# Sign bits of a weight block by a product with zero in bfloat16, and the mix's coefficient columns on GpSimd

## The chip, the core and the metric

The kernel runs on one core of a Trainium2 chip. The metric is the device time of one launch in microseconds; it took 817.42 us, the median of three runs (813.95 to 818.76). The engines are called PE (TensorE), DVE (VectorE), ACT (ScalarE), POOL (GpSimd) and SP (SyncE, which issues all DMAs here). Each engine takes its instructions strictly in the order of its own queue and waits on semaphores for the others.

## The reference

Eight batches, eight heads, 576 tokens, 64 features for a head. First a causal attention with a forgetting bias, then a channel mix over the 512 features of all heads:

```
bias   = min(-(cum_i - cum_j), 0), cum = cumsum(max(s, 0))
attn   = softmax(q k^T / 8 + bias, causal);  x = attn v, heads side by side
x_prev = x one token earlier
xk = mu_k x + (1 - mu_k) x_prev;  xr = mu_r x + (1 - mu_r) x_prev
out = sigmoid(xr w_r) * (relu(xk w_k)^2 w_v)
```

q, k, v, s and mu are float32; the three weights (512 x 1024, 1024 x 512, 512 x 512) are float64.

## The kernel before

**Attention.** A visit handles one batch and one pair of heads. The first visits (batch 0, cut in two tile groups A and Z) use plain float32 products; from batch 1 on each float32 operand is split in two parts, and POOL makes most of these parts (KH, KL, QL and G tiles, lines 1132 to 1165). Visits of batches 0 and 1 turn the softmax weights on PE, later visits turn float16 parts by DMA.

**Weights.** `load_weight` (line 813) brings a block of 128 rows and 512 columns of a weight into SBUF as raw float64 words; there are 8 blocks of w_k, 4 of w_r and 8 of w_v. A float32 is then put together from bits. Line 855 (POOL) makes the upper exponent bits from the top byte of each word, as the even 16-bit halves of a tile `last3`; line 863 (POOL) makes the sign bit as the odd halves; line 871 (ACT) and line 876 (DVE) bring the lower part into PSUM and clamp it, with the row maximum beside it; line 883 (DVE) shifts it, combines it with `last3` by a bitwise or, and has the float32 block. `split` then writes two float16 halves: the high one on ACT (line 894) or POOL (line 899), the low one on DVE (line 907) or, in two instructions, on POOL (lines 913 and 917).

**Coefficients.** The mix uses float16 halves too, so its operands are scaled. `set_range(w)` (line 701, w = 0 for k and 1 for r) multiplies mu and 1 − mu by the row maxima (`shares`, line 706), finds their maximum over all partitions through PE, and makes `mu_late` (line 738), the columns that later batches use. `set_group_mu(g, w)` (line 768) makes `group_mu` (named mu_g, line 770) for token groups 0 to 2, from `shares`, `ranges` and the group's `scale`. Each is a tile of 128 partitions and 4 or 8 elements. The readers of mu_g are the mix lines 1877 to 1893 of the first chunks, the readers of mu_late lines 1520 and 1530.

**Channel mix.** 18 chunks of 256 tokens each: mixed operands in a ring, hidden products (line 1949), the gate (line 2012), the output products (line 2057).

**The order of the work.** Nothing is emitted directly. Every operation becomes a task with an engine, a time that the program's own table gives it (`dve`, `act`, `pool`, `pe`, `dma`, lines 390 to 423: elements times a rate plus an extra), and the buffers that it reads and writes. Some tasks carry an alternative on another engine (`or_pool`, `or_dve`, `or_act`). `Plan.run` (line 322) plays a list schedule forward and backward 60 times and keeps the order with the shortest planned end; so a changed engine or a changed number for one task can move tasks on all engines. Until the first split attention product the plan puts filler matmuls (line 450) where PE would have nothing to do.

Of the kernel before, what the change touches and what calls it, by code (L numbers as in the profile page):

```python
# [337 lines left out]
def forgetting_attention_then_channel_mix(  # L338
# [362 lines left out]
    def set_range(w):  # L701
        name = "kr"[w]
        x = most[name]
        for y in range(2):
            dve(
                lambda y=y: nc.vector.tensor_tensor(
                    out=shares.ap[:, w, y], in0=mu.ap[:, w, y], in1=x.ap[:, :, 2], op=ALU.mult
                ),
                [(mu, w), (mu, 2)] + [(x, (c, "m")) for c in range(NC)], [(shares, (w, y))], NC,
            )  # L710
        dve(
            lambda: nc.vector.tensor_reduce(
                out=tops.ap[:, w : w + 1], in_=shares.ap[:, w].rearrange("p y c -> p (y c)"),
                axis=mybir.AxisListType.X, op=ALU.max, apply_absolute_value=True,
            ),
            [(shares, (w, 0)), (shares, (w, 1))], [(tops, w)], 2 * NC,
        )
        ps = spread(lambda: tops.ap[:, w : w + 1], (tops, w))

        def own(i):  # L720
            return ranges.ap[:, w, i : i + 1]

        dve(
            lambda: nc.vector.tensor_reduce(
                out=own(0), in_=ps.get()[:, 0:P], axis=mybir.AxisListType.X, op=ALU.max,
            ),
            [ps], [(ranges, w)], P,
        )
        dve(power(lambda: own(1), lambda: own(0), False), [(ranges, w)], [(ranges, (w, "p"))], 1)
        dve(  # L730
            lambda: nc.vector.tensor_scalar(
                out=own(1), in0=own(1), scalar1=4.0, scalar2=None, op0=ALU.mult,
            ),
            [], [(ranges, (w, "p"))], 1,
        )
        dve(lambda: nc.vector.reciprocal(own(2), own(1)), [(ranges, (w, "p"))], [(ranges, (w, "i"))], 1)
        dve(
            lambda: nc.vector.tensor_scalar(
                out=mu_late.ap[:, w], in0=shares.ap[:, w], scalar1=own(2), scalar2=1.0 / HALF,
                op0=ALU.mult, op1=ALU.mult,  # L740
            ),
            [(ranges, (w, "i")), (shares, (w, 0)), (shares, (w, 1))], [(mu_late, w)], 2 * NC,
        )

    def set_scale(g, tops_of, keys):
# [20 lines left out]
        dve(lambda: nc.vector.reciprocal(own(1), own(0)), [(x, 0)], [(x, 1)], 1)  # L766

    def set_group_mu(g, w):
        dve(
            lambda: nc.vector.tensor_scalar(  # L770
                out=group_mu[g].ap[:, w], in0=shares.ap[:, w], scalar1=ranges.ap[:, w, 2:3],
                scalar2=scale[g].ap[:, 1:2], op0=ALU.mult, op1=ALU.mult,
            ),
            [(ranges, (w, "i")), (shares, (w, 0)), (shares, (w, 1)), (scale[g], 1)],
            [(group_mu[g], w)], 2 * NC,
        )

    def set_gate(g):
# [34 lines left out]
    def load_weight(name, c, o, w, due, x):  # L813
# [34 lines left out]
        top = most[name]  # L848
        column = top.ap[:, c, o : o + 1] if name != "v" else top.ap[:, c : c + 1]

        def short(i):
            return last3.get().bitcast(mybir.dt.int16)[:, i:1024:2]

        pool(
            lambda: nc.gpsimd.tensor_scalar(
                out=short(0),
                in0=words.get().bitcast(mybir.dt.uint8)[:, 3 : 4096 : 8],
                scalar1=1.0 / 32.0, scalar2=-31.0 / 64.0, op0=ALU.mult, op1=ALU.add,
            ),
# [1 line left out]
        )  # L861
        pool(
            lambda: nc.gpsimd.tensor_scalar(
                out=short(1),
                in0=words.get().bitcast(mybir.dt.int16)[:, 3 : 2048 : 4],
                scalar1=32768.0, scalar2=0.0, op0=ALU.mult, op1=ALU.min,
            ),
            [words], [(last3, 1)], 512, 210, 1.0,
        )
# [20 lines left out]
        def split(unit_at, key):  # L890
# [28 lines left out]
                    op=ALU.subtract,  # L919
                )  # L920

            or_pool(dve(low, [whole, key, hi], [lo], 512, extra=260), low_in_two, 512, 1551)
            if name == "v":
                or_dve(
                    act(
# [1442 lines left out]
```

## Time and profile before

| | |
|---|---|
| median of three runs | 817.42 us |
| profiled execution | 817.64 us |
| its span, from first to last instruction | 815.8 us |
| PE busy | 754.2 us (92%) |
| DVE busy | 607.2 us (74%) |
| ACT busy | 568.6 us (70%) |
| POOL busy | 518.3 us (64%) |

Busy shares are means over the whole span. The profile also cuts the span in stretches and gives the busy time, the number of instructions and the granted clock of PE in each; the stretch shows which engine has no idle time left there. A chain of waits is followed back from the last instruction, at each step to whatever released it, so it names the work on which the end depended. Matmuls are pipelined and their ends are modelled, so a nearly full PE can still hold gaps.

### The profile page before, as it was taken

The page shows a single profiled execution, that of the slowest core. Times are in us where ns is not written, and L with a number is a line of the kernel's source. Part 1 is how long each engine was busy: PE and PEld are TensorE (multiplying, and loading weights), DVE is VectorE, ACT ScalarE, POOL GpSimd, SP SyncE. Part 2 cuts the span into 40 slices and gives each one's busy share as a digit, 9 for nine tenths or more (in the row PEclk, how much of TensorE's full clock was granted, in tenths as well). Part 3 has the DMA queues.
Part 4 walks back from the last instruction along what each step waited for, and adds up shares of the span by engine and source line. Part 5 has one row for each costly group of instructions (what it writes and reads, how often), then busy time and mean ns, then how long its engine had stood idle before and what let it go on. Part 6 is the DMA issues. An engine that isn't in the chain of part 4 may idle for free.

```text
span 815.8 us, 16987 instructions
## 1 busy us (share of the span) xinstructions
PE 754.2 (92%) x5400; PEld 503.8 (62%) x5400; DVE 607.2 (74%) x1825; ACT 568.6 (70%) x1716; POOL 518.3 (64%) x606
## 2 busy tenths in 40 slices
PE   9868888879899999998999899999999999999998
PEld 8645666557465666565666565757575656656664
DVE  8757886777998799988888978887887878423321
ACT  6656886757698689978797788887787878312211
POOL 8995999665745658966977598648966873010000
PEclk9989997889999999999999999999999999999999
DMA  8634555415564898897879777958787755300000
GB/s 262 209 100 133 161 173 179 131 43 145 130 127 103 174 158 180 172 202 132 181 167 191 139 183 166 185 122 172 145 184 137 131 110 83 76 14 14 27 27 27
DMA packets 207337, 109.93 MB, mean 135 GB/s; under 512 B 178000, under 2 KB 183888, under 8 KB 207248
## 3 DMA queue, kind: packets, MB, share of 16 engines
q1 hardware_dynamic: 207248, 108.85, 58.7%
q8 instruction: 43, 0.70, 0.4%
q14 instruction: 46, 0.38, 0.2%
HBM read 54.09 MB, written 12.24 MB: 81 GB/s over the span
## 4 chain that ended last, share of the span: by engine, by line
PE 52%; DVE 19%; ACT 11%; POOL 8%; issue 6%; DMA 2%; SPq 1%; DVEq 0%; ACTq 0%; POOLq 0%
PE m L2057 16%; PE m L1949 8%; PE m L2012 7%; PE pp L1475 3%; PE s L1289 3%; DVE W L1347 3%; PE t L1289 2%; ACT W L1341 2%; PE s L1216 2%; PE pp L1699 2%; PE pp L2057 2%; ACT t L1316 2%; PE t L1594 2%; PE t L1949 2%; ACT s L1316 2%
## 5 line engine op out<-in xcount | busy, mean ns | idle before, releaser
L1949 PE MATMUL m<-xkh,w_k 128*128 128x256 f16 x1008 | 188.4, 276 | 9.0 <-DVE kl L1999 8.0
L1949 PEld LDWEIGHTS <-w_k 128*128 128x128 f16 x1728 | 162.8, 99 | 43.2 <-issue 16.5
L2057 PE MATMUL m<-w_v,kh 128*128 128x512 f16 (+1 forms) x544 | 169.3, 377 | 2.5 <-ACT g L2026 1.3
L1949 PE MATMUL m<-xkl,w_k 128*128 128x256 f16 x504 | 139.2, 276 | 0.0
L2057 PE MATMUL m<-w_v,kl 128*128 128x512 f16 (+1 forms) x272 | 102.7, 378 | 1.6 <-DVE w_v L931 1.2
L1136 POOL TENSOR_TENSOR KH<-raw,KH 64x576 fp32r<-64x576 f32 x64 | 91.1, 1424 | 10.4 <-issue 4.7
L2057 PEld LDWEIGHTS <-kh 128*128 128x128 f16 x592 | 56.7, 98 | 65.4 <-issue 12.5
L2031 POOL TENSOR_SCALAR g<-g,scale 128x512 f32<-128x512 f32 x29 | 22.2, 765 | 104.8 <-ACT g L2026 100.2
L1160 POOL TENSOR_TENSOR QL<-raw,G 64x576 fp32r<-64x576 f32 (+1 forms) x64 | 84.5, 1320 | 3.8 <-ACT G L1149 1.0
L2012 PE MATMUL m<-w_r,xrh 128*128 128x512 f16 x240 | 79.6, 391 | 7.7 <-DVE kl L1999 5.2
L1316 ACT ACTIVATE s<-s,nm 128x64 f32<-128x64 f32 (+2 forms) x144 | 61.6, 428 | 27.8 <-DVE nm L1301 24.8
L1347 DVE SCALAR_TENSOR_TENSOR W<-s,rinv,W 128x64 f16<-128x64 f32 (+2 forms) x144 | 65.1, 456 | 14.4 <-ACT W L1341 13.5
L1341 ACT ACTIVATE W<-s,rinv 128x64 f16<-128x64 f32 (+2 forms) x144 | 64.7, 454 | 12.9 <-DVE rinv L1332 11.1
L1289 PE MATMUL s<-KH,G 128*128 128x64 f32 (+3 forms) x192 | 68.9, 362 | 4.0 <-DVE W L1347 3.6
L1962 ACT ACTIVATE r<-m 128x512 f32<-128x512 f32 x61 | 36.5, 598 | 50.8 <-PE m L1949 50.8
L1347 DVE SCALAR_TENSOR_TENSOR W<-t,rinv,W 128x512 f16<-128x512 f32 (+1 forms) x96 | 61.6, 645 | 8.3 <-ACT W L1341 7.7
L1289 PE MATMUL s<-KL,QL 67*128 67x64 f32 (+3 forms) x192 | 67.3, 355 | 0.0
L1156 POOL CAST G<-raw 128x576 fp32r<-128x576 f32 x48 | 31.8, 662 | 52.5 <-issue 24.6
L1316 ACT ACTIVATE t<-t,nm 128x320 f32<-128x320 f32 (+1 forms) x96 | 55.3, 576 | 6.0 <-DVE nm L1378 3.7
L1301 DVE CUSTOM_DVE_ANT_0 t<-t,lower 128x512 f32<-128x512 f32 (+1 forms) x96 | 57.1, 601 | 2.2 <-PE t L1289 1.4
L1341 ACT ACTIVATE W<-t,rinv 128x512 f16<-128x512 f32 (+1 forms) x96 | 57.8, 608 | 1.2 <-DVE rinv L1332 1.1
L1475 PE MATMUL pp<-T,V 128*64 128x512 f16 (+6 forms) x768 | 54.4, 295 | 0.0
(250 smaller groups left out, 1981.2 us busy)
## 6 DMA issues: line engine op xcount, KB each, us to landing
raw<-in_q SPq DMA_DIRECT2D x112, 144.0 KB
raw<-in_k SPq DMA_DIRECT2D x32, 288.0 KB
vn<-in_v SPq DMA_DIRECT2D x24, 384.0 KB
out<-g SPq DMA_DIRECT2D x35, 256.0 KB
wd<-in_moe_w_v SPq DMA_DIRECT2D x8, 512.0 KB
T<-W SPq DMA_TRANSPOSE x192
V<-in_v SPq DMA_DIRECT2D x8, 320.0 KB
wd<-in_moe_w_k SPq DMA_DIRECT2D x4, 512.0 KB
```

The source lines that it names most:

```text
L1136: lambda own=own, other=other, K=K: nc.gpsimd.tensor_tensor(out=K.get()[other], in0=k.get()[own], in1=f32(K.get()[own]), op=ALU.subtract),
L1160: lambda x=x, QQ=QQ, QL=QL: nc.gpsimd.tensor_tensor(out=QL.get()[0:64, 0:nq], in0=x.get()[0:64], in1=f32(QQ.get()[0:64]), op=ALU.subtract,),
L1289: lambda x=x, G=G, K=K, r=r: nc.tensor.matmul(ps.get()[:m, :n], G.get()[:r, q : q + m], K.get()[:r, k0 : k0 + n], start=x == 0, stop=x == 1,),
L1301: lambda: nc.vector.tensor_tensor_reduce(out=ps.get()[:, :n], in0=ps.get()[:, :n], in1=mask(), scale=-SCALE, scalar=3.0e38, op0=ALU.add, o ...
L1316: lambda: nc.scalar.activation(ps.get()[:, :n], ps.get()[:, :n], AF.Exp, bias=nm.get()[:, i + o : i + o + 1], scale=-1.0, accum_out=sums.g ...
L1341: lambda: nc.scalar.activation(part(0), ps.get()[:, :n], AF.Copy, scale=rinv.get()[:, i : i + 1]),
L1347: lambda: nc.vector.scalar_tensor_tensor(out=part(1), in0=ps.get()[:, :n], scalar=rinv.get()[:, i : i + 1], in1=part(0), op0=ALU.mult, op1 ...
L1475: nc.tensor.matmul(ps.get()[64 * j : 64 * j + 64, a:e], V.get()[:, block[0], block[1], j], moving(j), start=first, stop=last, tile_positio ...
L1949: lambda u=u, f=f, c=c, n=n, w=w, x=x: nc.tensor.matmul(ps.get()[:, u * CT : (u + 1) * CT], weight["k", c, f // 4].get()[:, w, f % 4 * P : ...
L1962: lambda: nc.scalar.activation(r.get(), ps.get(), AF.Relu, scale=2.0**-52),
L2012: lambda c=c, n=n, x=x, w=w: nc.tensor.matmul(ps.get(), chunk(1, x, ch).get()[:, c, ts], weight["r", c, 0].get()[:, w], start=c == 0 and n ...
L2057: lambda f=f, i=i, x=x, w=w, ps=ps, columns=columns: nc.tensor.matmul(ps.get()[:, 0:n], x.get()[:, f, ts], weight["v", f, 0].get()[:, w, c ...
```

## The change

The sign bits come from another instruction. Before, POOL read the top 16 bits of each word as int16, multiplied by 32768 and took the minimum with 0, which leaves −32768 (only the sign bit set) for a negative number and 0 otherwise. Now POOL reads the upper 32 bits of each word as a float32, multiplies by 0.0 and writes bfloat16: a negative number gives minus zero, which is the sign bit alone. The tile and the places written are the same. The `shares`, `mu_late` and `mu_g` columns, twelve instructions in all, are tasks of POOL instead of DVE, with an extra of 200. The planner's number for the low half on DVE goes from 260 to 450 (plus 512 elements).

```diff
--- before.py
+++ after.py
@@ -702,11 +702,11 @@
         name = "kr"[w]
         x = most[name]
         for y in range(2):
-            dve(
-                lambda y=y: nc.vector.tensor_tensor(
+            pool(
+                lambda y=y: nc.gpsimd.tensor_tensor(
                     out=shares.ap[:, w, y], in0=mu.ap[:, w, y], in1=x.ap[:, :, 2], op=ALU.mult
                 ),
-                [(mu, w), (mu, 2)] + [(x, (c, "m")) for c in range(NC)], [(shares, (w, y))], NC,
+                [(mu, w), (mu, 2)] + [(x, (c, "m")) for c in range(NC)], [(shares, (w, y))], NC, 200,
             )
         dve(
             lambda: nc.vector.tensor_reduce(
@@ -734,12 +734,12 @@
             [], [(ranges, (w, "p"))], 1,
         )
         dve(lambda: nc.vector.reciprocal(own(2), own(1)), [(ranges, (w, "p"))], [(ranges, (w, "i"))], 1)
-        dve(
-            lambda: nc.vector.tensor_scalar(
+        pool(
+            lambda: nc.gpsimd.tensor_scalar(
                 out=mu_late.ap[:, w], in0=shares.ap[:, w], scalar1=own(2), scalar2=1.0 / HALF,
                 op0=ALU.mult, op1=ALU.mult,
             ),
-            [(ranges, (w, "i")), (shares, (w, 0)), (shares, (w, 1))], [(mu_late, w)], 2 * NC,
+            [(ranges, (w, "i")), (shares, (w, 0)), (shares, (w, 1))], [(mu_late, w)], 2 * NC, 200,
         )
 
     def set_scale(g, tops_of, keys):
@@ -766,13 +766,13 @@
         dve(lambda: nc.vector.reciprocal(own(1), own(0)), [(x, 0)], [(x, 1)], 1)
 
     def set_group_mu(g, w):
-        dve(
-            lambda: nc.vector.tensor_scalar(
+        pool(
+            lambda: nc.gpsimd.tensor_scalar(
                 out=group_mu[g].ap[:, w], in0=shares.ap[:, w], scalar1=ranges.ap[:, w, 2:3],
                 scalar2=scale[g].ap[:, 1:2], op0=ALU.mult, op1=ALU.mult,
             ),
             [(ranges, (w, "i")), (shares, (w, 0)), (shares, (w, 1)), (scale[g], 1)],
-            [(group_mu[g], w)], 2 * NC,
+            [(group_mu[g], w)], 2 * NC, 200,
         )
 
     def set_gate(g):
@@ -848,12 +848,9 @@
         top = most[name]
         column = top.ap[:, c, o : o + 1] if name != "v" else top.ap[:, c : c + 1]
 
-        def short(i):
-            return last3.get().bitcast(mybir.dt.int16)[:, i:1024:2]
-
         pool(
             lambda: nc.gpsimd.tensor_scalar(
-                out=short(0),
+                out=last3.get().bitcast(mybir.dt.int16)[:, 0:1024:2],
                 in0=words.get().bitcast(mybir.dt.uint8)[:, 3 : 4096 : 8],
                 scalar1=1.0 / 32.0, scalar2=-31.0 / 64.0, op0=ALU.mult, op1=ALU.add,
             ),
@@ -861,9 +858,8 @@
         )
         pool(
             lambda: nc.gpsimd.tensor_scalar(
-                out=short(1),
-                in0=words.get().bitcast(mybir.dt.int16)[:, 3 : 2048 : 4],
-                scalar1=32768.0, scalar2=0.0, op0=ALU.mult, op1=ALU.min,
+                out=last3.get().bitcast(BF16)[:, 1:1024:2], in0=word(1),
+                scalar1=0.0, scalar2=1.0, op0=ALU.mult, op1=ALU.mult,
             ),
             [words], [(last3, 1)], 512, 210, 1.0,
         )
@@ -919,7 +915,7 @@
                     op=ALU.subtract,
                 )
 
-            or_pool(dve(low, [whole, key, hi], [lo], 512, extra=260), low_in_two, 512, 1551)
+            or_pool(dve(low, [whole, key, hi], [lo], 512, extra=450), low_in_two, 512, 1551)
             if name == "v":
                 or_dve(
                     act(
```

The lines of the new file are lower by up to four behind the change: 855 is now 852, 863 is 860, 899 is 895, 907 is 903, 913 is 909, 917 is 913, 1054 to 1062 are 1050 to 1058, 1132 is 1128, 1136 is 1132, 1142 is 1138, 1156 is 1152, 1160 is 1156.

First place: POOL's queue where the blocks of w_r are put together. Before:

```order
L855 TENSOR_SCALAR w_r_00_597<-wd_262 128x512
L913 TENSOR_SCALAR xrh_286<-xrh_286,unit 128x512
L917 TENSOR_TENSOR w_k_10_593<-xrh_286,w_k_10_593 128x512
L855 TENSOR_SCALAR w_r_00_643<-wd_210 128x512
L863 TENSOR_SCALAR w_r_00_643<-wd_210 128x512
L863 TENSOR_SCALAR w_r_00_597<-wd_262 128x512
L855 TENSOR_SCALAR w_r_00_686<-xrl_319 128x512
L863 TENSOR_SCALAR w_r_00_686<-xrl_319 128x512
L855 TENSOR_SCALAR w_r_00_709<-xrl_319 128x512
L863 TENSOR_SCALAR w_r_00_709<-xrl_319 128x512
L913 TENSOR_SCALAR xrh_286<-xrh_286,unit 128x512
L917 TENSOR_TENSOR w_k_00_705<-xrh_286,w_k_00_705 128x512
```

And in the changed order, at the same work:

```order
L852 TENSOR_SCALAR w_r_00_581<-wd_246 128x512
L860 TENSOR_SCALAR w_r_00_581<-wd_246 128x512
L706 TENSOR_TENSOR shares<-mu,most_k 128x4 x2
L852 TENSOR_SCALAR w_r_00_601<-wd_210 128x512
L860 TENSOR_SCALAR w_r_00_601<-wd_210 128x512
L852 TENSOR_SCALAR w_r_00_629<-xrl_288 128x512
L860 TENSOR_SCALAR w_r_00_629<-xrl_288 128x512
L909 TENSOR_SCALAR xrh_276<-xrh_276,unit 128x512
L913 TENSOR_TENSOR w_k_00_593<-xrh_276,w_k_00_593 128x512
L852 TENSOR_SCALAR w_r_00_685<-xrl_288 128x512
L860 TENSOR_SCALAR w_r_00_685<-xrl_288 128x512
L1156 TENSOR_TENSOR QL_137<-raw_614,G_693 64x256
```

Before, two sign-bit instructions (863) of w_r stand behind three other weight tasks in a bunch; now every sign-bit instruction (860) directly follows its exponent instruction (852), and the two `shares` columns of k stand between the first and the second block of w_r.

Second place: the mu_g columns of group 2 (`mu_g_92`). Before, on DVE, behind the reciprocal of its scale:

```order
L766 RECIPROCAL scale_83<-scale_83 128x1
L1999 SCALAR_TENSOR_TENSOR kl_1172<-kh_1162,m_316 128x512
L1347 SCALAR_TENSOR_TENSOR W_2196<-s_163,rinv_2301,W_2196 128x192
L1347 SCALAR_TENSOR_TENSOR W_2196<-t_300,rinv_2301,W_2196 128x512
L1981 SCALAR_TENSOR_TENSOR m_215<-m_215,r_107 128x512
L770 TENSOR_SCALAR mu_g_92<-shares,ranges,scale_83 128x8
L1301 ISA s_163,nm_249<-s_163,corners_mask 128x64
L1301 ISA nm_249 128x1
L1347 SCALAR_TENSOR_TENSOR W_2196<-s_168,rinv_2301,W_2196 128x64
```

In the changed order, on POOL (1050 to 1058 split the values v in two parts, 1128 to 1156 the keys and queries):

```order
L1050 TENSOR_SCALAR vn_972<-vn_972,scale_84 128x768
L1050 TENSOR_SCALAR vn_1007<-vn_1007,scale_84 128x768
L1056 CAST V_2322<-vn_972 128x768
L1056 CAST V_2337<-vn_1007 128x768
L1058 TENSOR_TENSOR V_2322<-vn_972,V_2322 128x768
L1058 TENSOR_TENSOR V_2337<-vn_1007,V_2337 128x768
L1128 CAST KH_847<-raw_659 64x576
L1138 CAST KL_815<-raw_659 64x576
L1152 CAST G_817<-raw_644 128x576
L1132 TENSOR_TENSOR KH_847<-raw_659,KH_847 64x576
L770 TENSOR_SCALAR mu_g_92<-shares,ranges,scale_83 128x8 x2
L1156 TENSOR_TENSOR QL_148<-raw_644,G_817 64x576
```

Before, the first column stood five instructions behind its reciprocal on DVE, and the second 27 rows later; now both stand next to each other on POOL, behind the split of two value tiles and four instructions on keys and queries.

## Rows read from the trace of the kernel before

**Rows 1.** Busy time of each engine (instructions), granted clock, DMA share, GB/s, in five stretches.

```profile
core 0: us, PE busy (x) PEld busy (x) DVE busy (x) ACT busy (x) POOL busy (x), PEclk, DMA share, GB/s
0.00:60.00 60.00, 46.89 (x357) 37.98 (x358) 41.18 (x161) 37.15 (x121) 55.70 (x76) 0.92 0.61 194
60.00:145.00 85.00, 72.06 (x526) 54.51 (x526) 64.35 (x203) 64.76 (x185) 71.42 (x72) 0.90 0.52 159
145.00:220.00 75.00, 62.36 (x435) 42.33 (x434) 58.16 (x162) 48.39 (x150) 47.27 (x69) 0.89 0.42 110
220.00:700.00 480.00, 462.85 (x3346) 298.29 (x3344) 412.91 (x1256) 391.89 (x1220) 335.79 (x382) 1.00 0.75 153
700.00:816.00 116.00, 110.04 (x742) 70.66 (x740) 30.57 (x45) 26.37 (x43) 8.09 (x10) 1.00 0.08 26
```

**Rows 2.** The same for PE, of the filler line L450 alone.

```profile
0.00:60.00 60.00, 13.88 (x98) 10.61 (x99) 0.92 0.61 194
```

**Rows 3.** Chain that ended last, from 0 to 60 us, shares by line.

```profile
by line: POOL w_k L863 21.3%; POOL w_r L863 13.9%; POOL w_k L855 9.6%; DMA wd<-in_moe_w_k 8.7%; issue 8.0%; PE pp L450 5.9%; POOL w_k L917 5.8%; POOL w_r L855 5.7%; SPq L2179 3.6%; POOL xrh L913 3.4%; POOL QL L1160 2.2%; SPq L1070 1.9%; PE 
```

**Rows 4.** The same chain, from 60 to 150 us; below, one piece: start us, us.

```profile
by line: PE s L1216 12.3%; PE pp L1699 10.2%; PE t L1594 8.6%; PE m L1949 7.7%; issue 5.6%; DVE W L1231 5.5%; PE t L1699 5.4%; POOL w_v L863 4.7%; DVE am L1025 3.6%; PE m L2012 3.6%; POOL QL L1160 3.3%; POOL KH L1136 3.1%; ACT W L1250 2.8%;
...
84.07 1.38 DVE mu_late L738 x2
```

**Rows 5.** The same chain between 195 and 230 us, one piece.

```profile
by line: PE m L2012 20.4%; PE m L2057 20.4%; DVE mu_g L770 11.8%; PE m L1949 8.7%; PE pp L1699 7.4%; PE t L1289 4.1%; PE s L1289 3.9%; PE t L1699 2.9%; ACT W L1341 2.5%; ACT g L2026 2.0%; DVE m L1981 2.0%; ACT s L1316 1.7%; DVE t L1301 1.7%
```

**Rows 6.** Waits of DVE, 0 to 60 us: total us, times, longest us.

```profile
DVE xrh L883 <- POOL w_r L863: 6.1, 2, 4.2
DVE xrh L883 <- POOL w_k L863: 5.5, 7, 1.5
```

**Rows 7.** Waits of PE, same stretch and columns.

```profile
PE pp L450 <- DVE xrh L883: 5.9, 2, 4.6
```

**Rows 8.** Busy time of line L863 on POOL, by stretch.

```profile
0.00:60.00 60.00, 25.41 (x12) 0.92 0.61 194
60.00:145.00 85.00, 16.88 (x8) 0.90 0.52 159
```

**Rows 9.** Line L863: tile, count, ns min/median/max, first and last start us, forms.

```profile
L863 POOL TENSOR_SCALAR w_v<-wd x8: 2085/2106/2155, 85.4 to 137.9; 128x512 int16<-128x512 int16 x8
```

**Rows 10.** Lines L855 and L899 on POOL, columns as in group 9.

```profile
L855 POOL TENSOR_SCALAR w_v<-wd x8: 762/774/784, 68.2 to 137.0; 128x512 int16<-128x512 uint8 x8
L899 POOL TENSOR_SCALAR w_k<-xrh,unit x1: 682/682/682, 17.8 to 17.8; 128x512 f16<-128x512 f32 x1
```

**Rows 11.** Lines L706 and L738 on DVE, columns as in group 9.

```profile
L706 DVE TENSOR_TENSOR shares<-mu,most_k x2: 151/438/724, 38.7 to 39.4; 128x4 f32<-128x4 f32 x2
L706 DVE TENSOR_TENSOR shares<-mu,most_r x2: 155/156/157, 54.3 to 54.4; 128x4 f32<-128x4 f32 x2
L738 DVE TENSOR_SCALAR mu_late<-shares,ranges x2: 219/774/1328, 84.0 to 85.2; 128x8 f32<-128x8 f32 x2
```

**Rows 12.** Line L770 on DVE: busy us in total, mean ns, idle us before.

```profile
L770 DVE TENSOR_SCALAR mu_g<-shares,ranges,scale 128x8 f32<-128x8 f32 x6 | 6.5, 1099 | 0.0
```

**Rows 13.** POOL in order of time, 204 to 213 us: start us, us, instruction.

```profile
205.22 1.78 POOL L1054 TENSOR_SCALAR vn<-vn,scale 128x768 f32<-128x768 f32 x2
206.96 1.59 POOL L1060 CAST V<-vn 128x768 f16<-128x768 f32 x2
208.52 3.23 POOL L1062 TENSOR_TENSOR V<-vn,V 128x768 f16<-128x768 f32 x2
```

**Rows 14.** DVE in order of time, 207 to 213 us.

```profile
207.58 4.20 DVE L770 TENSOR_SCALAR mu_g<-shares,ranges,scale 128x8 f32<-128x8 f32 x1
```

**Rows 15.** Line L785 on POOL, columns as in group 9.

```profile
L785 POOL TENSOR_SCALAR scale<-scale,ranges x9: 258/264/582, 127.0 to 638.6; 128x1 f32<-128x1 f32 x9
```

**Rows 16.** Waits of POOL, 60 to 220 us.

```profile
POOL scale L785 <- DVE scale L761: 3.8, 1, 3.8
```

**Rows 17.** Line L907 on DVE, columns as in group 9.

```profile
L907 DVE SCALAR_TENSOR_TENSOR w_k<-xrh,unit,w_k x3: 742/991/1721, 19.3 to 41.9; 128x512 f16<-128x512 f32 x3
```

## The prediction

> **What bounds the kernel now.** I first read the busy times by stage [rows 1]. From 220 to 700 us PE is busy 462.9 of 480 us and from 700 on 110.0 of 116, at a granted clock of 1.00: there PE alone sets the pace, and nothing that POOL or DVE saves there is worth anything. The first 220 us are different. PE is busy 46.9 of the first 60 us, and 13.9 of those are fillers [rows 2], matmuls that compute nothing; from 60 to 145 us it is busy 72.1 of 85, from 145 to 220 us 62.4 of 75. POOL is the full engine: 55.7 of 60 and 71.4 of 85 us. So a microsecond saved early ends as nearly a microsecond saved, because the PE-bound part behind it only starts earlier.
>
> Second, the chain of waits, by stage. In the first 60 us the sign-bit line L863 holds 21.3% + 13.9% = 35.2%, that is 21.1 us [rows 3]. From 60 to 150 us it holds 4.7% of 90 us, 4.2 us, and the two mu_late columns stand on the chain with 1.38 us [rows 4]. Around 208 us one small column instruction holds 11.8% of 35 us, 4.1 us [rows 5]. Third, the waits agree with the chain: DVE stood 6.1 + 5.5 us waiting for L863 [rows 6], and PE, with only fillers left, 5.9 us for the DVE line behind it [rows 7].
>
> **(a) The sign bits.** 20 instructions on POOL stay 20. They cost 25.41 us (12 of them) before 60 us and 16.88 us (8) after [rows 8], 2.106 us each [rows 9]. The trace has no product with a bfloat16 output on POOL, so I bound the new price: below by 0.682 us, a product of the same length from float32 to float16 without strides, above by 2.106 us, the old form. The nearest row is L855, 0.774 us: the same 512 elements, read every 8 bytes and written every 4, as here [rows 10]. Nothing excludes a price between; I take 0.774. POOL then saves 25.41 − 12 × 0.774 = 16.1 us and 16.88 − 8 × 0.774 = 10.7 us. On the chain, the share 1 − 0.774/2.106 = 0.63 goes: 13.3 us of 21.1 and 2.7 of 4.2.
>
> Not all 13.3 us arrive, since something else is late next. POOL's first stage falls to about 40 us, and DVE is busy 41.2 us of the same 60 [rows 1]; two engines that hand blocks to each other cannot both be full at 41. I take three quarters, 10.0 us. The lower end is 5.9 us, what PE itself waited [rows 7], the upper 16.1. After 60 us I take 2.5 us, between 0 and 10.7.
>
> The first order piece, in the part on the change, shows the same place: before, the sign bits of the w_r blocks come late and in a bunch; now each follows its exponent line, and two shares columns stand between them.
>
> **(b) The small columns.** Twelve instructions leave DVE. They held it 2 × 0.438 + 2 × 0.156 + 2 × 0.774 = 2.7 us [rows 11] plus 6.5 us for the six mu_g [rows 12], and 1.4 + 4.1 us of that is on the chain. The 4.1 us is no work: POOL ran six instructions without a gap from 205.22 to 211.75 us [rows 13], and the mu_g that DVE began at 207.58 us ended at 211.78 [rows 14], with that run, while the faster mu_late, a column of the same size, took 0.219 us [rows 11]. The Trainium skill's page SBUF — State Buffer (Who interferes with whom) says that GpSimd and certain VectorE instructions, a tensor_scalar within SBUF among them, lock one shared pair of ports for a whole instruction and the later one blocks; the trace agrees, 4.20 us. By that rule the wait would go with the move, a full 4.1 us gained.
>
> I don't credit it in full, because on POOL the same column waits in the queue instead. In the second order piece both mu_g of scale_83 stand behind the six instructions of that V split, 6.5 us, and behind four more of the next keys. Of 5.5 us on the chain I take 2.5; the ends are 5.5 gained and 6.5 lost (the run that it now stands behind, if its readers wait for all of it).
>
> On POOL a column costs about what its 128x1 kin does, 0.264 us [rows 15], so 12 × 0.3 = 3.6 us, with eight of them before 145 us: 2.4 us on a full engine. Half of it I put on the path, −1.2 us (ends 0 and −3.6). The page GPSIMD Engine Reference (Engine selection) sends elementwise work to VectorE as GpSimd is about twice slower; rows 11 and 15 agree for idle engines (0.156 against 0.264 us), and by it alone (b) would be a loss of some 1.3 us. That does not change the sum much, since VectorE's price here is its waiting.
>
> Each share also adds a step from DVE to POOL and back (unit, share, tops). In POOL's order the first pair stands before three more sign-bit pairs; if DVE's last k block is late, they all queue behind it, and DVE's next blocks behind them. I take −1.0 us; the ends are 0 and −4.2, the longest wait between the two engines in this stage [rows 6].
>
> POOL had one wait of the kind that a mu_g will now have, for DVE's scale: 3.8 us [rows 16]. It returns below as a rival.
>
> **(c) The planner's price of the low half on DVE, 260 to 450.** One instruction of this kind goes from POOL to DVE (13 to 14). On DVE it takes 0.74 to 1.72 us [rows 17]; its two POOL instructions disappear. Credit 0, ends ±2 us.
>
> **(d) The rest of the order.** All five queues are rewritten, and 89 fillers stand where 100 stood. From 220 to 700 us PE idles 17.1 us; a different order may move a quarter of it, ±4 us. Credit 0.
>
> **(e) The clock.** It was 0.92, 0.90 and 0.89 in the three early stages [rows 1], a mixture of 1.2 and 2.4 GHz, and stretches of PE idling stand in each. Denser work could give back at most 0.08 × 46.9 + 0.10 × 72.1 + 0.11 × 62.4 = 17.8 us; fewer fillers could also cost a little. Credit 0.
>
> Sum: 10.0 + 2.5 + 2.5 − 1.2 − 1.0 = 12.8 us. The profiled execution took 817.64 us (span 815.8), 0.2 above the median of the runs, so 817.6 − 12.8 = 804.8; I say 805.
>
> **Rivals.**
> 1. Much more arrives. For it: the planner reckoned L863 at 722 ns (512 × 1.0 + 210) and it took 2106; with the true price its order fits the chip. Against: DVE's 41 us. It would be 13.3 + 2.7 from (a), 5.5 from (b), a quarter of the clock's 17.8 (4.5), less 2.2: 23.8 us, so 794.
> 2. DVE takes over the first stage at once. Only PE's direct 5.9 us and the 2.5 of (b) come, less 2.2: 811.4. For it: DVE 41.2 of 60. Against: part of that 41.2 is itself waiting on POOL, L907 taking up to 1.72 us [rows 17].
> 3. The product is as slow as the old form: (a) is nothing, 2.5 − 2.2 remain, 817.3. For it: no row of this form; against: three product and scale forms lie at 0.68 to 0.77.
> 4. Slower: POOL's queue stands at the mu_g and mu_late columns. Eight of them wait for a DVE reciprocal or scale, with KH, KL, QL and w_v lines behind, which PE's scores need. At 3.8 us each [rows 16] four waits cost 15.2 us and the gain is gone; five give 817.6 − 12.8 + 19.0 = 823.8. Against: the planner put each behind other POOL work, so the scale is mostly there.
>
> **How the numbers follow.** The forecast of 805 (800 to 810 alone) gets 0.52, rival 1 0.16, rival 2 0.14, rival 3 0.09, rival 4 0.09. Differences under 0.5%, 4.1 us, can't be told from none here. Faster than 813.3: nearly all of the forecast, all of rival 1, three quarters of rival 2, in sum 0.77; slower than 821.5: most of rival 4, 0.08; the rest, 0.15, is the same. The range 792 to 817 leaves out rival 4, half of rival 3 and the far end of rival 1, a little under 2 in 10.
>
> **What would show it.** The new line at 0.7 to 0.8 us (rival 3: 2.1); POOL busy under 47 us of the first 60; PE's busy time without fillers in the first 60 us above 40 us (33.0 now); DVE's wait for sign bits under 4 us; mu_g on POOL under 0.5 us with idle time before it under 2 us. If the steady part from 220 us on differs by more than 4 us, or DVE turns out full in the first 50 us, the forecast is wrong in its step (d) or (a).

## The result, and the profile after

The changed kernel takes 783.86 us, the median of four runs (783.54 to 784.91); the kernel before took 818.09 us in four runs beside it. The ratio is 0.9593 [0.9557, 0.9628]. The forecast of 805 us was 21 us too long, and the result lies outside the range of 792 to 817 us. The profiled execution has a span of 782.1 us against 815.8.

The stages of the changed kernel up to 700 us, in the columns of [rows 1]:

```profile
0.00:60.00 60.00, 51.70 (x405) 41.86 (x406) 50.44 (x186) 44.85 (x144) 49.58 (x90) 0.97 0.72 222
60.00:145.00 85.00, 76.61 (x603) 57.60 (x603) 72.19 (x227) 73.39 (x219) 74.44 (x93) 0.98 0.57 169
145.00:220.00 75.00, 66.74 (x479) 45.55 (x477) 60.72 (x189) 56.10 (x176) 41.62 (x61) 0.95 0.54 122
220.00:700.00 480.00, 467.75 (x3399) 300.72 (x3398) 392.53 (x1184) 372.31 (x1146) 327.51 (x373) 1.00 0.73 148
```

In the first 220 us PE now does some 1487 matmuls instead of 1318 (sums of the first three rows here and in [rows 1], with 89 fillers in the one and 100 in the other). POOL is not idle for it: between 60 and 145 us it is busier than before, 74.4 against 71.4 us. DVE rose from 41.2 to 50.4 us in the first 60, ACT from 37.2 to 44.9. The granted clock is 0.97, 0.98 and 0.95, where it was 0.92, 0.90 and 0.89.

Where the gain lies is seen from the first output product, the line that multiplies `w_v` with the hidden values (columns as in [rows 9]; first the kernel before, then the changed one):

```profile
L2057 PE MATMUL m<-w_v,kh x544: 272/379/637, 152.7 to 812.4; 128*128 128x512 f16 x171, 128*128 128x256 f16 x11
L2053 PE MATMUL m<-w_v,kh x544: 272/379/632, 119.6 to 778.8; 128*128 128x512 f16 x171, 128*128 128x256 f16 x11
```

It starts at 119.6 us where it started at 152.7. From its first to its last start are 659.2 us now and 659.7 before. So all of the gain has been made by the time that the first output product starts, and nothing is gained behind it.

The page gives PE 739.5 us of busy time against 754.2. The span fell by 33.7 us; 14.7 of that is shorter PE busy time (some 1.4 of it 11 fewer instructions on the filler line) and 19.0 is less PE idle time.

The new sign-bit line, which answers to [rows 9]:

```profile
L860 POOL TENSOR_SCALAR w_v<-wd x8: 772/776/783, 62.0 to 106.4; 128x512 bf16<-128x512 f32 x8
```

and its busy time, which answers to [rows 8]:

```profile
0.00:60.00 60.00, 9.87 (x12) 0.97 0.72 222
60.00:145.00 85.00, 6.21 (x8) 0.98 0.57 169
```

From 25.41 + 16.88 us POOL comes down to 9.87 + 6.21. The small columns are now on POOL, a share at 0.20 us (L706) and a `mu_late` at 0.277 (L738). The `mu_g`, which answer to [rows 12]:

```profile
L770 POOL TENSOR_SCALAR mu_g<-shares,ranges,scale x6: 341/372/1013, 46.3 to 188.2; 128x8 f32<-128x8 f32 x6
```

Of the waits that the prediction feared, two are left. One is POOL's for DVE, from 0 to 220 us (columns as in [rows 6]):

```profile
POOL mu_g L770 <- DVE inverses L1273: 1.7, 1, 1.7
```

The other is DVE's for POOL, from 0 to 60 us:

```profile
DVE tops L712 <- POOL shares L706: 1.0, 1, 1.0
```

For sign bits DVE waits no more; its combining line (883 before, 879 now) has one wait left in this stage, which is for PE:

```profile
DVE xrh L879 <- PE pp L1695: 1.6, 1, 1.6
```

### The profile page after: what moved, and what is told of

Its sections match the earlier page's. It is cut to its first block, busy times and chain, and to the rows that moved or that the text cites. A ratio compares the mean times of both kernels' runs of the same rounds, so it can differ in the third digit from the quotient of the medians.

```text
span 782.1 us, 16949 instructions
## 1 busy us (share of the span) xinstructions
PE 739.5 (95%) x5389; PEld 495.4 (63%) x5389; DVE 596.7 (76%) x1814; ACT 565.0 (72%) x1711; POOL 497.8 (64%) x621
## 4 chain that ended last, share of the span: by engine, by line
PE 47%; DVE 21%; ACT 14%; issue 6%; DMA 1%; POOL 1%; SPq 0%; DVEq 0%; ACTq 0%; POOLq 0%
PE m L2053 14%; PE m L1945 9%; PE m L2008 5%; DVE W L1343 4%; PE s L1285 3%; PE pp L1471 2%; ACT W L1337 2%; ACT wd L1516 2%; ACT s L1312 2%; PE pp L2053 2%; ACT t L1312 2%; DVE s L1297 2%; DVE t L1297 2%; PE t L1945 2%; PE t L1285 2%
## 5 line engine op out<-in xcount | busy, mean ns | idle before, releaser
L1945 PE MATMUL m<-xkh,w_k 128*128 128x256 f16 x1008 | 185.1, 275 | 4.9 <-DVE kl L1995 2.8
L1285 PE MATMUL s<-KH,G 128*128 128x64 f32 (+2 forms) x192 | 69.4, 362 | 8.8 <-DVE W L1343 7.1
L2027 POOL TENSOR_SCALAR g<-g,scale 128x512 f32<-128x512 f32 x24 | 18.4, 765 | 93.2 <-ACT g L2022 91.3
L1312 ACT ACTIVATE s<-s,nm 128x64 f32<-128x64 f32 (+1 forms) x144 | 61.5, 427 | 21.7 <-DVE nm L1297 17.8
L1343 DVE SCALAR_TENSOR_TENSOR W<-s,rinv,W 128x64 f16<-128x64 f32 (+2 forms) x144 | 65.6, 457 | 11.5 <-ACT W L1337 10.6
L1285 PE MATMUL s<-KL,QL 67*128 67x64 f32 (+1 forms) x192 | 68.3, 357 | 0.0
L1312 ACT ACTIVATE t<-t,nm 128x512 f32<-128x512 f32 (+1 forms) x96 | 55.4, 577 | 15.3 <-DVE nm L1374 8.3
```

The costliest lines, as they stand in the source:

```text
L1285: lambda x=x, G=G, K=K, r=r: nc.tensor.matmul(ps.get()[:m, :n], G.get()[:r, q : q + m], K.get()[:r, k0 : k0 + n], start=x == 0, stop=x == 1,),
L1312: lambda: nc.scalar.activation(ps.get()[:, :n], ps.get()[:, :n], AF.Exp, bias=nm.get()[:, i + o : i + o + 1], scale=-1.0, accum_out=sums.g ...
L1343: lambda: nc.vector.scalar_tensor_tensor(out=part(1), in0=ps.get()[:, :n], scalar=rinv.get()[:, i : i + 1], in1=part(0), op0=ALU.mult, op1 ...
L1945: lambda u=u, f=f, c=c, n=n, w=w, x=x: nc.tensor.matmul(ps.get()[:, u * CT : (u + 1) * CT], weight["k", c, f // 4].get()[:, w, f % 4 * P : ...
```

## The experiments

Three explanations stood against each other. **Product**: the 27 us that the instruction saves on POOL shorten the path. **Columns**: DVE no longer stands behind POOL's runs. **Order**: the change makes the planner lay out all five queues anew, and that order is better, whatever the instructions do; it has a special form, **price**, found later. The planner reckoned the old sign-bit line at 512 + 210 = 722 ns and the chip took 2106 [rows 9], so its order was built on a wrong number, while the new line takes 776 ns and fits it. The change leaves the number at 722: the instruction came to fit it. Times below are medians, with the ratio to the kernel before, which was timed beside each (medians of 815.1 to 818.4 us), and its 95% interval; gains are worked out from the ratio.

**One part at a time.** First the product alone. Every row of every queue stands where it stood before; one instruction has another form.

```diff
-                out=short(1),
-                in0=words.get().bitcast(mybir.dt.int16)[:, 3 : 2048 : 4],
-                scalar1=32768.0, scalar2=0.0, op0=ALU.mult, op1=ALU.min,
+                out=last3.get().bitcast(BF16)[:, 1:1024:2], in0=word(1),
+                scalar1=0.0, scalar2=1.0, op0=ALU.mult, op1=ALU.mult,
```

> The kernel before with one edit: the sign bits by the bfloat16 product (0.774 us instead of 2.106). The planner's number for it is unchanged, so all five queues stand instruction for instruction as before. Theory A (the shorter POOL instruction is the whole gain; POOL's 27 us come back as a faster start, an earlier w_v and a higher PE clock): 786 to 793 us, clock in the first 220 us from 0.90 to about 0.96. Theory B (the new order is worth as much as the instruction): 803 to 807 us, what the prediction's term (a) gave. Theory C (the small columns, that blocked DVE for 4 us, carry it): above 805 us.

Measured: 798.43 us, 0.9768 [0.9728, 0.9807], so 19 us gained (16 to 22), between theory A and theory B and in the range of neither. The first three stages:

```profile
0.00:60.00 60.00, 51.77 (x424) 42.23 (x425) 48.26 (x194) 44.63 (x140) 48.67 (x86) 1.00 0.68 218
60.00:145.00 85.00, 73.14 (x553) 53.92 (x550) 68.37 (x210) 68.56 (x201) 64.53 (x80) 0.93 0.56 169
145.00:220.00 75.00, 66.72 (x438) 43.31 (x438) 60.65 (x174) 52.16 (x165) 45.18 (x63) 0.92 0.52 113
```

The order being the same, this run shows the clock's part too: PE's busy time on the whole page is 746.4 us against 754.2 for the same 5400 matmuls, so of the 17.7 us by which the span fell 7.8 are shorter busy time and 9.9 less idling. The 7.8 us fit the rise of the clock over [rows 1], which is an estimate: 0.08 × 46.9 + 0.03 × 72.1 + 0.03 × 62.4 = 7.8.

The other way round: the changed kernel's queues, row for row, with the old instruction in them.

```diff
-                out=last3.get().bitcast(BF16)[:, 1:1024:2], in0=word(1),
-                scalar1=0.0, scalar2=1.0, op0=ALU.mult, op1=ALU.mult,
+                out=last3.get().bitcast(mybir.dt.int16)[:, 1:1024:2],
+                in0=words.get().bitcast(mybir.dt.int16)[:, 3 : 2048 : 4], scalar1=32768.0, scalar2=0.0, op0=ALU.mult, op1=ALU.min,
```

> The changed kernel with one edit: the sign bits by the old int16 form, 2.1 us, in the changed kernel's order. Theory A: the gain goes, 812 to 818 us. Theory B: about half of the gain stays, 798 to 804 us. Theory C: 790 to 796 us.

Measured: 801.41 us, 0.981 [0.9774, 0.9845], in theory B's range. Without any of POOL's saving on the sign bits the new order, with the columns on POOL in it, still gains 15.5 us. PE's busy time fell here too, to 746.0 us (with 11 fewer fillers). The two add up: 19.0 + 15.5 = 34.5, and the whole change gave 33 to 34.

Then the two small parts, each planned anew: the columns on POOL as in the diff of the change,

> The kernel before with the twelve small columns on POOL alone (the queues are planned anew). Theory A: within 4 us of before, 813 to 821. Theory B: some 5 us from the new order, either way. Theory C: 800 to 808 us, since the 5.5 us of columns on the chain go and what follows gains too.

and the price of the low half on DVE, `extra=260` to `extra=450`, alone.

> The kernel before with the planner's number for the low half on DVE at 450 instead of 260 alone (the queues are planned anew, no instruction has another form). Theory A: within 4 us of before. Theory B: up to 10 us faster. Theory C: as before.

Measured: 806.98 us, 0.9866 [0.9822, 0.9911], and 811.52 us, 0.9927 [0.9901, 0.9953]. Both are faster, the first within theory C's range and the second as theory B had it, but both also carry a new order, so neither says what its edit is worth by itself. For the columns that was asked again with the order held: they are planned on DVE and stand at the same places, but the instruction goes to POOL (PE, ACT and SP keep their queues).

```diff
         dve(
-                lambda y=y: nc.vector.tensor_tensor(
+                lambda y=y: nc.gpsimd.tensor_tensor(
...
         dve(
-            lambda: nc.vector.tensor_scalar(
+            lambda: nc.gpsimd.tensor_scalar(
```

> The kernel before; the twelve columns are planned as DVE tasks as before and emitted on POOL at the same places, so PE, ACT and SP keep their queues row for row. Columns alone in a new order took 807. Theory D (DVE's blocked columns cost the time, the order does not matter): 806 to 809 us. Theory E (the 10 us came from the new order): 813 to 818 us.

Measured: 812.1 us, 0.9942 [0.9914, 0.9971], a gain of 5 us (2 to 7), between theories D and E. A `mu_g` takes 0.346 us there at the median, much as in the changed kernel, and the longest wait of POOL for one is 1.3 us. But DVE now waits for the shares:

```profile
DVE tops L712 <- POOL shares L706: 3.4, 1, 3.4
```

The product was split by stage as well, in before's order: for the twelve blocks of k and r, and for the eight of v (the diff of the first run under `if name != "v":` and under `if name == "v":`).

> The kernel before, in its own order, with the bfloat16 product for the 12 blocks of w_k and w_r alone; w_v keeps the old form. All 20 gave 18 us. Theory F (the last w_v block sets the end, some 667 to 679 us behind it in ten kernels so far): the start is faster by 11 to 14 us, but w_v still costs 2.1 us a block, so its last block comes 5 to 10 us earlier and the end with it, 806 to 811 us. Rival G (the start is what counts, the first split scores): 801 to 804 us.

> The kernel before, in its own order, with the bfloat16 product for the 8 blocks of w_v alone. Theory F: nothing changes before 85 us, the last w_v block comes 7 to 11 us earlier, and so does the end: 805 to 809 us. Rival G: within 3 us of before, since the start is as it was; or the 2.5 us of the prediction.

Measured: 802.53 us, 0.9834 [0.9796, 0.9872], and 812.55 us, 0.9939 [0.991, 0.9968]: 13.6 and 5.0 us, together 18.6, the 19.0 of both at once. The first is in rival G's range; the second is slower than theory F said.

**Is it this order, or any other?** A number was changed that means nothing: the extra of `am` on DVE from 120 to 124 ns. The planner breaks its ties differently and the order is new. The same nudge was made in the changed kernel, and another one in the kernel before (the extra in `set_gate`).

```diff
-            [vn], [(am, hp)], P * nk, extra=120,
+            [vn], [(am, hp)], P * nk, extra=124,
```

> The kernel before with a number that has no meaning here changed by 4 ns (the planner's extra for the maximum over v, 120 to 124): another order, the same instructions. It shows how far orders scatter. If the 10 us of the columns and the 5 us of the price are chance of the order, this moves by as much, either way: 805 to 825 us. If they are more than chance, it stays within 3 us of before.

> The changed kernel with the same meaningless number changed (120 to 124): a second draw of its order. If 784 is an ordinary draw for these instructions, 779 to 790 us; if the changed kernel's order is a lucky one, 790 to 800 us.

```diff
-            [(x, 0), (ranges, (1, "p"))], [(x, 2)], 1, 200,
+            [(x, 0), (ranges, (1, "p"))], [(x, 2)], 1, 210,
```

> The kernel before with another number that matters to nothing here (the planner's extra for the gate's scale column, 200 to 210 ns): a second draw of the order, with the same instructions. The first draw gave 806. If the order of before is an unlucky one, this too comes out faster, 800 to 812 us; if the first draw was lucky, 813 to 822 us.

Measured: 806.36 us, 0.9894 [0.9864, 0.9924]; 784.33 us, 0.9598 [0.9569, 0.9627]; 804.38 us, 0.9852 [0.9817, 0.9887]. A meaningless nudge gains 9 and 12 us on the kernel before and nothing on the changed one, as was expected if the order before was a poor one among its like. With the product put into the first nudged order, queues unchanged,

> The nudged kernel (120 to 124, 806 us) in its order, with the bfloat16 product. If product and order add up (0.977 and 0.989): 788 to 791 us. If the product's 18 us were large because the order of before suffered most from it: 793 to 798 us.

790.37 us were measured, 0.9678 [0.9643, 0.9712]; the product of the two single ratios is 0.9768 × 0.9894 = 0.9665. Order and product again add up, as expected.

Next, the due time from which the planner counts the v blocks, later in the changed kernel (62000 to 77000) and earlier in the kernel before (to 47000). It was meant to test whether the last block of `w_v` sets the end.

```diff
-    V0 = 62000.0
+    V0 = 77000.0
```

> The changed kernel with the planned time of the w_v blocks (V0) 15 us later, nothing else. In the six kernels so far the end came 674 to 679 us after the start of the last combining or of w_v (before: 141.5, changed: 109.5), whatever was edited. Theory F (the last w_v block sets the end, since the output products cannot start before all eight are in): the last block moves later and the end with it, end = last block + 675, about 795 to 800 us. Rival G (both are only signs of a start that is faster throughout): 782 to 787 us, as PE has other work until then.

```diff
-    V0 = 62000.0
+    V0 = 47000.0
```

> The kernel before (old sign bits, columns on DVE) with the planned time of the w_v blocks 15 us earlier. Theory F: last block near 125 to 130, end 675 us behind it, 800 to 806 us. Rival G: POOL is as full as before and the attention's parts come later instead, 814 to 822 us.

Measured: 791.49 us, 0.9704 [0.9676, 0.9733], between theory F and rival G, and 800.75 us, 0.9821 [0.9795, 0.9847], in theory F's range: there the last `w_v` combine came at 130.5 us instead of 141.5. The test was weak: 15 us of due time moved that combine of the changed kernel from 109.5 to 114.4 us only. And in the nudged changed kernel it came at 115.1 us with the same time of the whole. So that one block does not set the end by itself. What goes with the end more closely is the first output product: in all twenty kernels of this document its line ran 651 to 667 us from first to last start, while the first start lay between 119.6 and 172.3 us.

**The price.** The kernel before, with the old slow instruction, and one number of the planner changed: it is now told 512 + 1590 = 2102 ns.

```diff
-            [words], [(last3, 1)], 512, 210, 1.0,
+            [words], [(last3, 1)], 512, 1590, 1.0,
```

> The kernel before with the old sign bits, and the planner told their true time (512 x 1.0 + 1590 = 2102 ns instead of 722). Theory H (the order of before was a bad one because its price for POOL was wrong): at or below the two draws with a meaningless nudge, 798 to 804 us. Theory I (it is one draw among many, a true price does not matter): 804 to 816 us.

Measured: 789.16 us, 0.9665 [0.9631, 0.9698]: 27 us gained with no instruction made cheaper, more than theory H had expected (798 to 804 us). The old line still takes its time, and POOL is as full as before, but the others are not held up by it:

```profile
L863 POOL TENSOR_SCALAR w_v<-wd x8: 2105/2122/2150, 59.2 to 110.9; 128x512 int16<-128x512 int16 x8
```

```profile
0.00:60.00 60.00, 53.02 (x426) 43.98 (x427) 50.94 (x195) 47.03 (x149) 55.46 (x72) 0.97 0.74 230
60.00:145.00 85.00, 76.08 (x597) 56.72 (x597) 75.59 (x234) 75.04 (x222) 76.72 (x75) 0.98 0.54 159
145.00:220.00 75.00, 65.15 (x467) 43.94 (x466) 63.72 (x188) 56.65 (x175) 43.30 (x68) 0.95 0.53 127
```

These rows should be read beside [rows 1]: POOL 55.46 and 76.72 us where it was 55.70 and 71.42, yet PE does 426 and 597 matmuls where it did 357 and 526, with 103 fillers where there were 100. DVE's waits for the sign bits, 6.1 + 5.5 us in the first 60 us before [rows 6], are, from 0 to 145 us:

```profile
DVE xrh L883 <- POOL w_v L863: 2.9, 1, 2.9
DVE xrh L883 <- POOL w_k L863: 0.2, 1, 0.2
```

What the planner did with the true number is to give POOL less of the work that may go to either engine. Line 913, the first half of the low part made in two POOL steps, is left with one instruction (last; the other two are of the kernel before):

```profile
L913 POOL TENSOR_SCALAR xrh<-xrh,unit x6: 687/691/1122, 18.6 to 72.5; 128x512 f32<-128x512 f32 x6
L913 POOL TENSOR_SCALAR xrl<-xrl,span_v x1: 692/692/692, 169.2 to 169.2; 128x512 f32<-128x512 f32 x1
L913 POOL TENSOR_SCALAR xrh<-xrh,span_v x1: 692/692/692, 123.7 to 123.7; 128x512 f32<-128x512 f32 x1
```

There were seven of it before, and six or seven also in the two nudged kernels and in the new order with the old line, all planned with 722. Of the casts of the queries that ACT does otherwise, POOL has two (line 1152) where it had eight.

The same in the changed kernel: its columns, but the old instruction, and the true price for it.

```diff
-                out=last3.get().bitcast(BF16)[:, 1:1024:2], in0=word(1),
-                scalar1=0.0, scalar2=1.0, op0=ALU.mult, op1=ALU.mult,
+                out=last3.get().bitcast(mybir.dt.int16)[:, 1:1024:2],
+                in0=words.get().bitcast(mybir.dt.int16)[:, 3 : 2048 : 4], scalar1=32768.0, scalar2=0.0, op0=ALU.mult, op1=ALU.min,
...
-            [words], [(last3, 1)], 512, 210, 1.0,
+            [words], [(last3, 1)], 512, 1590, 1.0,
```

> The changed kernel with the old sign bits and their true time, 2102 ns, told to the planner. With the old form at the wrong price the changed kernel took 801, and the kernel before with the true price 789. Theory H (the price was the fault, the 27 us of POOL themselves cost little in an order that knows of them): 785 to 792 us. Theory I (789 was a lucky draw): 796 to 806 us.

Measured: 791.38 us, 0.97 [0.9661, 0.974]. Beside 801.41 us for the same instructions under the wrong price, that is 10 us; beside the changed kernel it is 7.5 us slower. This is theory H's range, and here too line 913 (909 in this kernel) is left with one instruction.

Then the prices of POOL's lines were brought nearer to what the trace of the changed kernel shows, 16 numbers by 32 to 165 ns (the sign-bit line's among them, from 722 to 774), to see whether a truer table does better still.

```diff
-            [words], [(last3, 1)], 512, 210, 1.0,
+            [words], [(last3, 1)], 512, 262, 1.0,
...
-            [(scale[g], 1)], [vn], n, 210,
+            [(scale[g], 1)], [vn], n, 260,
```

> The changed kernel with the planner's numbers of fourteen other POOL tasks brought to what the traces show (raised by 32 to 165 ns, for instance the exponent line from 722 to 774). If a truer price is worth something wherever it stands: 776 to 782 us. If only the one gross error, 722 for 2106, mattered: 781 to 788 us.

Measured: 790.16 us, 0.9673 [0.9628, 0.9718], 6 us slower than the changed kernel and slower than either expectation. The first output product starts as early as in the changed kernel (119.7 us); the 6 us were lost behind it. A truer table in small things is worth less than the scatter of the orders. No version beat the changed kernel.

**The clock.** To learn what the granted clock alone is worth, some 110 fillers were added between the first split scores and the first scores of batch 1, in both kernels, wherever PE was about to take up something that another engine had just made.

```diff
+            if a < n < e and on[i] == "PE" and any(on[d] != "PE" and n - place[d] < 25 for d in self.tasks[i][3]):
+                self.idle()
```

> The kernel before in its own order, with about 110 more filler matmuls on PE, each ahead of a PE task that has just been given its input by another engine, from the first split scores to the first scores of batch 1. Nothing useful is added or moved. Theory J (part of the gain was PE's clock, 0.90 in this stretch before and up to 0.98 after): clock from 0.90 to about 0.97 between 60 and 105 us, and 3 to 7 us faster, 810 to 814. Theory K (a fuller PE only follows from the faster start and its clock is worth little): 815 to 820 us, the fillers' own time on top.

> The changed kernel in its own order with the same kind of fillers. Its clock is 0.97 to 0.98 there already: both theories expect 783 to 787 us; below 782 the clock would still hold something.

Measured: 837.0 us, 1.0223 [1.0162, 1.0284], and 804.87 us, 0.9847 [0.9808, 0.9886], so some 19 and 21 us lost against the kernels without them, and all expectations missed. Both failed as tests of the clock. It did not rise: in the first of the two it was 0.90 between 60 and 145 us, as before. And the fillers themselves took a good deal of PE. Their line (454 there, columns as in [rows 2]) was busy, in the first of the two,

```profile
0.00:835.00 835.00, 42.12 (x211) 22.81 (x211) 0.97 0.58 132
```

where the 100 of the kernel before took 14.35 us, so 27.8 us more; in the other it was 37.13 against 11.53, 25.6 us more. They also write a tile `pp` that the mix shares, so ACT and DVE waited for them, from 60 to 105 us in the first of the two:

```profile
ACT pp L1883 <- PE pp L454: 5.6, 2, 3.3
DVE pp L1899 <- PE pp L454: 4.6, 5, 2.0
```

How much of the loss is the fillers' own time and how much these waits was not separated.

**All together.** The kernels fall in two groups, by whether the planner's number for the sign-bit line is near what the chip takes. The split and filler runs are left out.

| number and chip | runs, us |
|---|---|
| 722 for 2106 ns (wrong) | before 818.1, columns in the old order 812.1, low half's price 811.5, columns 807.0, nudges 806.4 and 804.4, the new order with the old line 801.4, v earlier 800.8: mean 807.7 |
| right, new line (0.78 us) | product in the old order 798.4, v later 791.5, product in the nudged order 790.4, POOL's prices 790.2, changed, nudged 784.3, changed 783.9 |
| right, old line (2.1 us) | before with the true price 789.2, changed with the old line and its true price 791.4 |

No kernel with the wrong number is under 800, none with a right one over 799. The eight right ones have a mean of 789.9. These 18 us are not the price alone, since six of the eight also have the faster instruction, and some of them have the same order as a wrong one. The kernels with the old line compare better: the eight with the wrong number, in seven orders, lie between 800.8 and 818.1, and the two that were planned with the true one at 789.2 and 791.4. Inside the last two groups old and new line can't be told apart by more than their scatter.

## Why the prediction was wrong, point by point

- **What bounds.** Right: PE's pace behind the early part is the same, 659 us from the first to the last output product, and the first 220 us hold the gain.
- **Term (a), the sign bits.** The duration was right: 0.776 us where 0.774 was taken. So were POOL's savings, 15.5 and 10.7 us where 16.1 and 10.7 stood. Its gain came out larger: with the order held the product gave 13.6 us in the k and r blocks and 5.0 in the v blocks, where 10.0 and 2.5 were credited. But 7.8 us of the 17.7 that the span fell in the run with all twenty blocks are shorter busy time of PE, which the prediction keeps apart as term (e); the 9.9 us of idle time that went are less than the 12.5 credited. So no run shows that the path's share itself was too small. The argument that two engines cannot both be full at 41 us was no bound: in that run POOL and DVE were both busy 48 to 49 us of the first 60, and PE did more. The order piece in which the sign bits were said to come in a bunch shows one of four away from its exponent line, that of `w_r_00_597`.
- **Term (b), the columns.** The sum of its three numbers was +0.3 us; with the order held they give 5 (2 to 7). The 4.20 us of [rows 14] are gone, and the feared 6.5 us did not come in their place: the longest wait of POOL for a `mu_g` is 1.7 us in the changed kernel. The step over the shares did cost something: DVE waited 3.4 us for them with the order held (1.0 in the changed kernel, just the credited loss), and the 5 us are what is left after that. So the full 5.5 us fits the first of the three numbers, and 2.5 looks too little. The Trainium skill's page SBUF — State Buffer (Who interferes with whom) would have it so: by its rule a tensor_scalar on VectorE can be blocked by a GpSimd instruction that holds the shared ports, and these are on VectorE no longer. The 4.20 us that went agree with it. The Trainium skill's page GPSIMD Engine Reference (Engine selection) puts GpSimd at about twice slower for operations with two inputs; a share, which is one, took 0.20 us against 0.156 on an idle DVE, 1.3 times as long, and the loss that the page suggests did not come. The 0.264 us that the prediction set beside 0.156 belongs to another instruction.
- **Term (c), the price of the low half.** It can't be told apart from a new order: 6 us alone, less than a nudge.
- **Term (d), the rest of the order.** This is the step that failed. It was credited 0 ± 4 us, from the 17.1 us that PE idles between 220 and 700 us. The order acts ahead of that, where PE idled 38.7 of 220 us. The new order with the old line gained 15.5 us; take off the columns' 5, and some 10 us remain, as much as the two nudges gave (9 and 12). With the product's 19 us and the columns' 5 as measured, and (d) still at nothing, the sum would be 793.6 us, within the range; the order's 10 us take it out. The sign set for this step, a steady part that differs by more than 4 us, looked at the part that did not change.
- **Term (e), the clock.** Also credited 0, with no other reason than that fewer fillers could cost a little, though 17.8 us stood as its upper bound. PE's busy time fell by 14.7 us, some 1.4 of it for fewer fillers. Both halves of the change have a part in it: 7.8 us with the product in the old order, 8.2 with the new order and the old line (746.0 against 754.2 us, fewer fillers included). This is not to be added to the 19, 5 and 10 us, which hold it already; how much sooner the kernel ends for it was not shown.
- **Rival 1** named the cause in a clause: the planner's 722 against 2106 ns. It was then priced without the order, as the sum of better terms, at 794 us and a chance of 0.16, and its objection (DVE's 41 us) was the argument of term (a) that proved no bound. The true price alone, with the slow line left as it was, gives 789 us. So 27 of the 34 us are to be had without POOL's 26 us of saved time: making the planner's number true by the table does much of what the new line does by the instruction. How much of the 27 is the price and how much a lucky draw of the order, two orders can't tell; both lie 9 us or more below the lowest of the eight kernels with the old line and the wrong number.
- **Rivals 2, 3 and 4** did not occur: DVE was not the bound, the product is fast, and POOL's queue did not stand at the columns.

Of the signs that the prediction named, one did not show. POOL was to fall under 47 us of the first 60 and stood at 49.6, with 90 instructions there instead of 76. PE's busy time without fillers is 51.7 − 11.5 = 40.2 us, just over the 40 that were asked (11.53 us of fillers, 89 instructions); DVE's wait for sign bits went; a `mu_g` took 0.37 us at the median, though one took 1.01.

What stays open: why the order before was poor even among those planned with the wrong number, and what the clock alone is worth. That the last `w_v` block and the first output product go with the end is a correlation and no cause that was shown.

## What to carry to other kernels

Compare each number of a planner's table with the duration in the trace before anything else: one was three times too low here, and putting it right, with the slow instruction left as it was, gained 27 us of 817 in one kernel and 10 in its sister, where making the instruction itself fast brought 19. When an edit goes through a planner, run it once with the order held, and nudge a meaningless number once or twice to see how far orders scatter (up to 1.5% here), before a gain is put down to the edit. A full engine need not become less busy for a kernel to gain: in the corrected kernel POOL stayed as full, and had other work.

## What the runs showed of the hardware

On POOL, 512 elements read at a stride of 8 bytes and written at 4 took 2.11 us as int16 to int16 (multiply, then minimum) and 0.776 us as float32 to bfloat16 (two multiplies); bytes to int16 took 0.774 [rows 10]. Which of the types or the minimum costs the difference was not tried. In the first run with fillers PE's granted clock was 1.00 up to 40 us, with PE busy 33.8 of 40 us, and 0.70, a mixture of 1.2 and 2.4 GHz, from 40 to 80 us, where the added fillers begin and PE was busy 30.2 of 40. In the kernel before the same stretches had 0.96 and 0.87, with PE busy 34.2 and 29.3 us. The two rows with fillers:

```profile
0.00:40.00 40.00, 33.81 (x263) 28.28 (x263) 28.95 (x102) 25.09 (x83) 35.80 (x58) 1.00 0.75 237
40.00:80.00 40.00, 30.17 (x181) 21.62 (x182) 21.53 (x93) 20.22 (x56) 31.13 (x31) 0.70 0.33 100
```
